# Chunked attention and a quadratic-ReLU network on one core: q and k of the first tiles loaded four tokens to a partition and turned in 64x64 blocks, the first stages in another order, copies of weights issued later

## The chip, the core and the metric

One NeuronCore of a Trainium2 chip runs the whole program. Its engines each work through a queue of their own: TensorE multiplies matrices (PE in the profile, its weight loads PEld), VectorE (DVE) and ScalarE (ACT) work element by element, GpSimd (POOL) and SyncE (SP) mostly issue DMAs. They wait for one another by semaphores. The metric is device time of one execution in microseconds (us), as the median over runs. Names in the profile leave buffer numbers out, so `q_sb` stands for both `q_sb0` and `q_sb1`.

## What is computed

```python
# q, k, v: (8, 8, 576, 64): batch, heads, tokens, head size; chunks of 64 tokens, 9 to a sequence
scores = scale * np.matmul(q_c, k_c.transpose(0, 1, 2, 4, 3))
scores = scores - np.max(scores, axis=-1, keepdims=True)
attn = np.exp(scores)
attn = attn / (np.sum(attn, axis=-1, keepdims=True) + 1e-09)
out = np.matmul(attn, v_c)
# x = the 8 heads side by side: (4608, 512); w_in (512, 2048), w_out (2048, 512)
h = x @ w_in
g = np.where(h >= 1, h, np.where(h <= -1, 0.0, (h + 1) ** 2 / 4))
return g @ w_out
```

Each token attends only to the 64 tokens of its own chunk. The weights come as 64-bit floats and are read as pairs of 32-bit words.

## The kernel before

The 4608 tokens are nine tiles of 512 (`t` = 0 to 8): the first 512 tokens of each of the eight sequences, and one tile (`t` = 6) of the eight last chunks. Attention handles two heads at a time, `g` = 0 to 3. The network goes through the hidden size in 16 steps `j` of 128.

**Network.** Every float32 operand of the large products is split into a high and a low part (`xh` and `xl`, `gh` and `gl`, two halves of `weight`), and three products take the place of one. `ffn_in(t, j)` is 12 matmuls of 128x512, `ffn_out(t, j)` is again 12, three for each of the four output banks. Tiles 0 to 2 go so. From tile 3 on the tiles go in pairs: `ffn_quad` computes the hidden layer of a pair with seven products of mixed operands for each two steps; it keeps one tile's result, and sends the other's to memory (`hold`), from where `recall` fetches it for the pair's second tile. The mixed weights are made in tiles 1 and 2 by `mix_weights` and written to memory by `to_mixed`, on the POOL queue. Three of the seven are plain parts of `weight` and need no arithmetic; the kernel before issues these three copies ahead of the arithmetic.

**Attention.** `attn_turn` transposes q and k of two heads, `scores_of` multiplies them in 64x64 blocks, `attn_softmax` subtracts the maximum, takes exp and divides by the sum; `attn_turn_back` transposes the result and `values_of` multiplies it with v; `attn_split` copies it into `xh` and `xl`. For `t` = 0, and for `g` = 0 and 1 of `t` = 1 (`by_row`), the turning is done on TensorE: `flip` is four transposes of 128x128 against an identity matrix into one bank, for q and then for k, and ACT copies each bank to memory on chip. Later tiles are turned on DVE. The loads of these early q and k (`load_rows`, `load_halves`) put one token of each chunk on a partition, so every piece of memory that a DMA reads is one token of one head, 64 floats or 256 bytes.

**Order.** Nothing is issued in the order of the code. `Plan.add` notes every piece of work with its engine, an assumed cost, and what it reads and writes. `Plan.emit` then plays it through, giving a free engine its ready piece of lowest rank, and so writes one fixed queue for each engine. Where TensorE would be idle in that play before the network starts, it adds fillers: multiplications of the identity with itself (L1105), into banks that are not in use yet. They are instructions like any other: once in the queue they run, whether or not TensorE would have had to wait. The whole queue of before has 45 fillers.

**First stages.** `first_loads` gives the order of the loads for `t` = 0, the k of `g` = 0 and 1 on the ACT queue and the rest on SP. A loop then turns, scores and normalises `g` = 0 to 3, with the way back and the values two steps behind. The weights of the first three steps are prepared (`prepare`: word pairs to high and low parts, three operations of ACT and three of DVE each) after that in rank.

**Outputs.** `store` copies a finished output bank to a buffer, by ACT for `s` = 0 and 2 and by DVE for `s` = 1 and 3, and SP sends it. From tile 2 on the buffers are the four `tmp`, taken in turn. `ffn_quad` takes from the same four for what `hold` sends to memory.

## Time and profile before

| what | value |
|---|---|
| runs | 829.47, 829.10, 827.03 us; median 829.1 |
| the profiled execution | 828.9 us, its span 827.1 us |
| granted TensorE clock | 1.000 |
| moved | 146.80 MB in 278683 packets, 243152 of them under 512 bytes |
| TensorE by lines | L700 about 582 us, L880 about 273 us, L665 about 203 us of summed durations, which overlap |
| work for the first attention tile | up to about 30 us |
| last matmul starts | 822.94 us |

Durations of neighbouring matmuls overlap, so what a matmul costs is read from the start of one to the start of the next. In rows of the timeline the columns are: start in us, us covered by the row, engine, line, operation, what it writes and reads, shape, number of records; and in brackets how long the engine sat idle before it and what ended that. A float32 matmul outside the transpose mode leaves two records in the trace (the first 12 fillers are x24).

### The profile page before, as it was taken

How to read it: one execution, taken by the hardware profiler on the slowest of the kernel's cores; microseconds unless marked ns; L12 is line 12 of the kernel's file. 1: busy time of each engine (PE TensorE's matmuls, PEld its weight loads, DVE VectorE, ACT ScalarE, POOL GpSimd, SP SyncE). 2: the span in 40 equal slices, each digit the busy share in tenths (PEclk: the TensorE clock that was granted, in tenths of full speed). 3: DMA queues.
4: the chain of work that ended last, by engine and by line, in shares of the span. 5: the costliest groups of instructions: out<-in, count | busy, mean ns of one | idle time of the engine just before them, and what ended most of it. 6: DMA issues, size and time to landing. Idle time of an engine off the chain costs nothing.

```text
span 827.1 us, 15446 instructions
## 1 busy us (share of the span) xinstructions
PE 819.0 (99%) x5786; PEld 676.7 (82%) x5786; DVE 563.2 (68%) x965; ACT 422.5 (51%) x723; POOL 153.8 (19%) x278
## 2 busy tenths in 40 slices
PE   9999999999999999999999999999989999999998
PEld 8778878888888888888888888888878888888886
DVE  4889998857778888786787748775756254454422
ACT  5899965444445465455464344544544254454422
POOL 1222112222221111112122111121122121121220
PEclk9999999999999999999999999999999999999999
DMA  9998886554697546979597738875663264552432
GB/s 203 285 314 294 247 195 156 137 124 101 170 242 150 124 102 175 260 179 262 167 226 231 175 108 214 216 190 188 164 223 95 63 207 157 168 169 86 157 98 77
DMA packets 278683, 146.80 MB, mean 177 GB/s; under 512 B 243152, under 2 KB 251600, under 8 KB 278608
## 3 DMA queue, kind: packets, MB, share of 16 engines
q1 hardware_dynamic: 251584, 61.25, 33.7%
q0 software_dynamic: 24768, 83.90, 31.0%
q10 hardware_dynamic: 2256, 0.66, 0.5%
q8 instruction: 46, 0.75, 0.4%
q14 instruction: 29, 0.24, 0.1%
HBM read 101.71 MB, written 36.70 MB: 167 GB/s over the span
## 4 chain that ended last, share of the span: by engine, by line
PE 88%; DMA 4%; issue 2%; DVE 2%; SPq 2%; POOL 1%; ACT 0%; ACTq 0%; POOLq 0%; DVEq 0%
PE ps_o L700 43%; PE ps_h L880 26%; PE ps_h L665 13%; PE ps_a L478 2%; PE ps_h L496 2%; PE ps_a L700 1%; DMA words_wo<-in_moe_w_out_dram 1%; DMA v_sb<-in_v_dram 1%; DMA q_sb<-in_q_dram 1%; SPq L409 1%; DMA held<-tmp 1%; SPq L359 1%; DMA k_sb<-in_k_dram 1%; PE ps_a L436 0%; PE ps_o L665 0%
## 5 line engine op out<-in xcount | busy, mean ns | idle before, releaser
L700 PE MATMUL ps_o<-parts_wo,gh 128*128 128x512 f32 x1120 | 347.9, 392 | 2.2 <-DVE tmp L727 2.2
L700 PEld LDWEIGHTS ps_o<-parts_wo,gh 128*128 128x128 f32 x1120 | 208.6, 188 | 46.2 <-DVE tmp L727 2.8
L700 PE MATMUL ps_o<-parts_wo,gl 128*128 128x512 f32 x560 | 218.4, 390 | 0.0
L880 PE MATMUL ps_h<-big_wi,big_wi 128*128 128x512 f32 x720 | 172.3, 389 | 0.0
L880 PEld LDWEIGHTS ps_h<-big_wi,big_wi 128*128 128x128 f32 x720 | 135.2, 188 | 28.0
L665 PE MATMUL ps_h<-xh,parts_wi 128*128 128x512 f32 x376 | 125.4, 394 | 0.1
L686 DVE TENSOR_TENSOR gl<-r,gh 128x512 fp32r<-128x512 f32 x120 | 82.4, 687 | 60.9 <-ACT gh L685 60.1
L700 PEld LDWEIGHTS ps_o<-parts_wo,gl 128*128 128x128 f32 x560 | 105.2, 188 | 22.4 <-DVE gl L686 0.3
L685 ACT CAST gh<-r 128x512 fp32r<-128x512 f32 x120 | 74.2, 619 | 96.0 <-PE ps_o L700 55.8
L811 POOL DMA_DIRECT2D big_wi<-mixed x84 | 44.9, 535 | 264.1 <-PE ps_h L880 251.7
L665 PEld LDWEIGHTS ps_h<-xh,parts_wi 128*128 128x128 f32 x376 | 70.6, 188 | 16.1 <-DVE r L676 0.5
L665 PE MATMUL ps_h<-xl,parts_wi 128*128 128x512 f32 x188 | 73.6, 391 | 0.4 <-DVE xl L614 0.4
L894 ACT ACTIVATE tmp<-big_wi 128x512 f32<-128x512 f32 x48 | 30.3, 632 | 71.4 <-DVE big_wi L889 70.0
L880 PE MATMUL ps_h<-xh,big_wi 128*128 128x512 f32 x192 | 63.5, 390 | 0.0
L672 ACT ACTIVATE r<-ps_h 128x512 f32<-128x512 f32 x47 | 27.9, 597 | 43.6 <-PE ps_h L665 43.4
L889 DVE TENSOR_TENSOR big_wi<-ps_h,big_wi 128x512 f32<-128x512 f32 x48 | 32.9, 685 | 19.0 <-PE ps_h L880 13.8
L898 DVE SCALAR_TENSOR_TENSOR tmp<-big_wi,tmp 128x512 f32<-128x512 f32 x48 | 33.2, 692 | 15.9 <-ACT tmp L897 15.8
L676 DVE SCALAR_TENSOR_TENSOR r<-ps_h,r 128x512 f32<-128x512 f32 x47 | 32.1, 682 | 16.1 <-ACT r L675 15.9
L880 PEld LDWEIGHTS ps_h<-xh,big_wi 128*128 128x128 f32 x192 | 36.1, 188 | 7.7 <-DVE e L889 0.2
L665 PEld LDWEIGHTS ps_h<-xl,parts_wi 128*128 128x128 f32 x188 | 35.3, 188 | 7.7 <-DVE xl L614 0.7
L761 POOL DMA_DIRECT2D mixed<-e x32 | 17.2, 543 | 127.2 <-ACT e L790 127.2
L904 POOL DMA_DIRECT2D held<-tmp x48 | 26.4, 550 | 72.6 <-DVE tmp L898 72.5
(150 smaller groups left out, 1030.9 us busy)
## 6 DMA issues: line engine op xcount, KB each, us to landing
big_wi<-mixed POOLq DMA_DIRECT2D x84, 512.0 KB, 4.0
held<-tmp POOLq DMA_DIRECT2D x48, 256.0 KB, 3.8
words_wi<-in_moe_w_in_dram SPq DMA_DIRECT2D x16, 512.0 KB, 6.6
words_wo<-in_moe_w_out_dram SPq DMA_DIRECT2D x16, 512.0 KB, 7.5
out_dram<-tmp SPq DMA_DIRECT2D x31, 256.0 KB, 3.3
aT_both<-qT_both SPq DMA_DIRECT2D x112, 64.0 KB, 2.8
v_sb<-in_v_dram SPq DMA_DIRECT2D x52, 128.0 KB, 3.7
q_sb<-in_q_dram SPq DMA_DIRECT2D x104, 64.0 KB, 3.5
```

What stands on the lines that cost most here:

```text
L665: nc.tensor.matmul(out=ps, lhsT=weight["wi", j][:, half, kc * P:(kc + 1) * P], rhs=x, start=(kc == 0 and i == 0), stop=(kc == KC - 1 and i ...
L672: plan.add("act", 0.48, lambda: nc.scalar.activation(out=r, in_=ps, func=AF.Relu, bias=0.5, scale=0.5), (pkey,), (rkey,))
L676: plan.add("dve", 0.6, lambda: nc.vector.scalar_tensor_tensor(out=r, in0=ps, scalar=1.0, in1=r, op0=ALU.max, op1=ALU.min), (pkey,), (rkey,))
L685: plan.add("act", 0.52, lambda: nc.scalar.copy(out=gh, in_=r), (rkey,), (ghkey,))
L686: plan.add("dve", 0.6, lambda: nc.vector.tensor_tensor(out=gl, in0=r, in1=gh.bitcast(F32), op=ALU.subtract), (rkey, ghkey), (glkey,), port ...
L700: nc.tensor.matmul(out=acc, lhsT=x[:, cols], rhs=weight["wo", j][:, half, :], start=(j == 0 and i == 0), stop=(j == NF - 1 and i == 2),)
L811: plan.add("pool", 0.65, lambda: nc.gpsimd.dma_start(out=place_of(f"wi{slot}").bitcast(F32), in_=mixed[u]), keys, (f"wi{slot}_0", f"wi{slo ...
L880: nc.tensor.matmul(out=bank, lhsT=w[:, c:c + P], rhs=x()[:, kc, :], start=start and kc == 0 and k == 0, stop=kc == 1 and k == 2, skip_grou ...
L889: plan.add("dve", 0.6, lambda: nc.vector.tensor_tensor(out=out(), in0=bank, in1=x(), op=ALU.add), (key, xkey), (out_key,))
L894: plan.add("act", 0.5, lambda: nc.scalar.activation(out=r, in_=h(), func=AF.Relu, bias=0.5, scale=0.5), (hkey,), (rkey,))
L898: plan.add("dve", 0.6, lambda: nc.vector.scalar_tensor_tensor(out=r, in0=h(), scalar=1.0, in1=r, op0=ALU.max, op1=ALU.min), (hkey,), (rkey,))
L904: plan.add("pool", 0.65, lambda: nc.gpsimd.dma_start(out=held[j], in_=r), (rkey,), (f"held{j}",), lag=2.1, moving=0.8)
```

## The change

**Loading and turning.** For the tiles of `by_row`, `load_rows` now loads q and k of two heads in one DMA: partition `p` gets tokens 4p to 4p + 3 of both heads, so pieces of 1024 bytes. `flip_rows` turns q and k together by 32 multiplications of 64x64 blocks with a 64x64 piece of the identity, into a pair of banks. One copy for each of q and k then puts the tokens back in order: it reads the bank in order and writes every fourth element. Two of the eight copies of `t` = 0 (k of `g` = 0 and 1) are DVE's, the others ACT's. v of `t` = 0 and of the first half of `t` = 1 goes in two DMAs as other tiles do.

**Order.** The loop over the first stages is replaced by `in_turn`, a list written out; softmax is cut in two (`attn_exp`, `attn_norm`), and the preparing of the first weights stands in the list. `first_loads` is reordered, and k of `g` = 0 and 2 goes on ACT's queue. Softmax and the turn back of later bursts get 22 places less of priority (`plan.behind`).

**Late copies and one buffer.** `mix_weights` issues its three plain copies after the arithmetic. `store` puts bank `s` = 3 of tiles 3, 5 and 7 into the one `e` buffer instead of a `tmp`.

```diff
+        rows = src[BATCH[t], 2 * g:2 * g + 2, :T, :].rearrange("h (p r) d -> p h (r d)", r=NS)
+        queue.dma_start(out=dst.rearrange("p (h e) -> p h e", h=2), in_=rows)
...
+    def flip_rows(pair, q_rows, k_rows):
+        for r in range(NS):
+            for n, x in enumerate((q_rows, k_rows)):
+                for a in range(2):
+                    for h in range(2):
+                        rows, at = slice(a * C, (a + 1) * C), h * HALF + r * D
+                        to = n * HALF + r * C
+                        nc.tensor.matmul(
+                            out=pair[h * D:(h + 1) * D, a, to:to + C],
+                            lhsT=x[rows, at:at + D], rhs=ident[rows, rows], start=True, stop=True,
+                        )
...
-            plan.add("pe", 0.45, lambda src=src, ps=ps: flip(ps, src), (skey,), pkeys, columns=T,
-                     lag=0.0)
-            copy = plan.add(
-                "act", 0.48, lambda ps=ps, dst=dst: nc.scalar.copy(out=dst, in_=ps),
+        plan.add("pe", 0.75, lambda: flip_rows(pair, *(src for (_, src), _ in sides)),
+                 [skey for (skey, _), _ in sides], pkeys, columns=1024, lag=0.0)
+        for n, (_, (dkey, dst)) in enumerate(sides):
+            by_dve = (t, g, n) in COPIED
+            eng = nc.vector.tensor_copy if by_dve else nc.scalar.copy
+            turned[n] = plan.add(
+                "dve" if by_dve else "act", 0.6 if by_dve else 0.48,
+                lambda n=n, dst=dst, eng=eng: eng(
+                    out=dst.rearrange("p (a u r) -> p a r u", a=2, r=NS),
+                    in_=pair[:, :, n * HALF:(n + 1) * HALF].rearrange("p a (r u) -> p a r u", r=NS),
+                ),
                 pkeys, (dkey,), lag=late(t, 1.5),
             )
...
+            elif t >= PAIRED and (t - PAIRED) % 2 == 0 and s == NS - 1:
+                okey, o = e_bufs[0]
...
-        ("q", 0), ("k", 0), ("q", 1), ("k", 1), ("q", 2), ("k", 2), ("wi", 0), ("q", 3), ("k", 3),
-        ("v", 0), ("v", 1), ("wi", 1), ("v", 2), ("v", 3),
+        ("q", 0), ("k", 0), ("q", 1), ("k", 2), ("k", 1), ("q", 2), ("wi", 0), ("v", 1),
+        ("q", 3), ("k", 3), ("v", 0), ("wi", 1), ("v", 2), ("v", 3),
...
+    in_turn = (
+        "T0 S0 A0 T1 S1 N0 A1 N1 T2 S2 B0 V0 T3 S3 A3 A2 X0 B1 V1 N2 X1 B2 N3 B3 "
+        "V2 V3 W0 W2 X2 X3 W1"
+    )
...
+        plan.behind = 22
         for at in then:
             attn_softmax(*at)
         if then:
             attn_turn_back_pair(then)
+        plan.behind = 0
```

In the list, T turns q and k, S makes scores, A is maximum to exp, N is the sum and the division, B turns back, V makes values, X splits, and W prepares weights.

What this does to the queues is seen at three places. First the start of TensorE's queue. The names `q_sb`, `first_wi` and so on are buffers of q and k, `ps_o` and `ps_a` banks, `kT` and `qT_both` the turned tiles. Before:

```order
L1105 MATMUL ps_h_107<-ident 128x128 x12
L436 MATMUL ps_o_106<-ident,k_sb_72 128x128 x4
L1105 MATMUL ps_h_107<-ident 128x128
L436 MATMUL ps_o_105<-ident,q_sb_70 128x128 x4
L1105 MATMUL ps_h_107<-ident 128x128 x4
L478 MATMUL ps_a<-kT_78,qT_both 64x64 x16
L436 MATMUL ps_o_106<-ident,k_sb_73 128x128 x4
L436 MATMUL ps_o_105<-ident,q_sb_71 128x128 x4
L1105 MATMUL ps_h_107<-ident 128x128 x4
L478 MATMUL ps_o_103<-first_wo_116 64x64 x16
```

After, on the same engine from the same place (three more pairs of L439 rows follow each pair shown):

```order
L1130 MATMUL ps_h_106<-ident 128x128 x11
L439 MATMUL ps_o_103<-ident,q_sb_70 64x64 x4
L439 MATMUL ps_o_103<-ident,k_sb_72 64x64 x4
...
L1130 MATMUL ps_h_106<-ident 128x128 x5
L493 MATMUL ps_a<-kT_78,qT_both 64x64 x16
L439 MATMUL ps_o_103<-ident,q_sb_71 64x64 x4
L439 MATMUL ps_o_103<-ident,k_sb_73 64x64 x4
...
L1130 MATMUL ps_h_106<-ident 128x128 x8
L493 MATMUL ps_o_104<-first_wo_115 64x64 x16
```

Eight transposes have become 32 block products for each `g`, one burst instead of two, and the scores of one `g` stand directly ahead of the turning of the next. The fillers are 49 in the whole queue, 11 of them ahead of the first turning.

Second, ACT's queue where the last attention results of the first tile are copied (`first_wi` under L581 and L601 takes `aT`, the turned-back softmax of `g` = 2 and 3; `words_wo` is the first block of `w_out` as loaded). Before:

```order
L581 COPY first_wi_113<-ps_o_106 128x512
L613 CAST xh_0_85<-ps_o_103 128x2x4x64
L338 CAST parts_wi_455<-tmp_101 128x512
L613 CAST xh_0_87<-ps_a 128x2x4x64
L320 ACTIVATE tmp_102<-words_wi_353 128x512
L326 ACTIVATE words_wi_353<-words_wi_353 128x512
L581 COPY first_wi_113<-ps_o_106 128x512
L320 ACTIVATE tmp_99<-words_wo_355 128x512
```

After:

```order
L321 ACTIVATE tmp_101<-words_wi_355 128x512
L633 CAST xh_0_85<-ps_o_104 128x2x4x64
L327 ACTIVATE words_wi_355<-words_wi_355 128x512
L321 ACTIVATE tmp_99<-words_wo_365 128x512
L601 COPY first_wi_112<-ps_o_103 128x512
L327 ACTIVATE words_wo_365<-words_wo_365 128x512
L339 CAST parts_wi_552<-tmp_102 128x512
L601 COPY first_wi_112<-ps_o_103 128x512
```

The first reading of `words_wo` stood behind the last of these copies and now stands ahead of both.

Third, DVE's queue at the end of tile 5 (L898 and L921 end what `hold` sends off, L727 and L749 are `store`). Before:

```order
L898 SCALAR_TENSOR_TENSOR tmp_99<-big_wi_161,tmp_99 128x512
L686 TENSOR_TENSOR gl_97<-r_93,gh_95 128x512
L727 COPY tmp_101<-ps_o_106 128x512
L686 TENSOR_TENSOR gl_98<-big_wi_161,gh_96 128x512
L727 COPY tmp_99<-ps_o_103 128x512
L686 TENSOR_TENSOR gl_97<-r_94,gh_95 128x512
```

After:

```order
L921 SCALAR_TENSOR_TENSOR tmp_102<-big_wi_160,tmp_102 128x512
L706 TENSOR_TENSOR gl_98<-r_94,gh_96 128x512
L706 TENSOR_TENSOR gl_97<-r_93,gh_95 128x512
L749 COPY tmp_100<-ps_o_103 128x512
L749 COPY e_80<-ps_o_104 128x512
L706 TENSOR_TENSOR gl_98<-big_wi_160,gh_96 128x512
```

The second copy of an output bank went into the buffer of the last held result, `tmp_99`; now it goes into `e_80`, and stands directly behind the first.

More of the change, by code (lines that the diff above doesn't have):

```diff
@@ L238, in bank_pair @@
         return psum.tile([P, 2, T], F32, name=name)
-    o_pair, a_pair = bank_pair("ps_o23"), bank_pair("ps_a")
-    o_banks = buffers(psum, "ps_o", 2) + [(f"ps_o{2 + b}", o_pair[:, b, :]) for b in range(2)]
+    o_pairs, a_pair = [bank_pair("ps_o01"), bank_pair("ps_o23")], bank_pair("ps_a")
+    o_pair = o_pairs[1]
+    o_banks = [(f"ps_o{b}", o_pairs[b // 2][:, b % 2, :]) for b in range(4)]
     a_banks = [(f"ps_a{b}", a_pair[:, b, :]) for b in range(2)]
@@ L355, in load_rows, with by_half @@
     def load_rows(dst, src, t, g, queue):
-        dst = dst.rearrange("p (c d) -> p c d", d=D)
-        for j in range(2):
-            queue.dma_start(
-                out=dst[j * C:(j + 1) * C],
-                in_=heads_rows(src, t, 2 * g + j).rearrange("c p d -> p c d"),
-            )
-    def load_halves(dst, src, t, g, queue):
-        dst = dst.rearrange("p (u r d) -> p u r d", r=2, d=D)
-        for j in range(2):
-            rows = heads_rows(src, t, 2 * g + j).rearrange("(r u) p d -> r p u d", r=2)
-            for r in range(2):
-                queue.dma_start(out=dst[j * C:(j + 1) * C, :, r, :], in_=rows[r])
+        rows = src[BATCH[t], 2 * g:2 * g + 2, :T, :].rearrange("h (p r) d -> p h (r d)", r=NS)
+        queue.dma_start(out=dst.rearrange("p (h e) -> p h e", h=2), in_=rows)
     def by_row(t, g):
         return t < TURNED or t == TURNED and g in ROWED
+    def by_half(t, g):
+        return t == TURNED and g not in ROWED
     def load_blocks(dst, src, t, g, queue):
@@ L464, in attn_turn @@
             if t == 0:
-                turned[n] = copy
+                ended[0] = turned[n]
     def scores_of(t, g):
@@ L475, in product @@
             rows = slice(half * C, (half + 1) * C)
-            at = i * HALF + n * C if t == TURNED and not by_row(t, g) else (2 * n + i) * C
+            at = (i * HALF + n * C if by_half(t, g)
+                  else (n // 2 * 4 + 2 * i + n % 2) * C if by_row(t, g) else (2 * n + i) * C)
             at = slice(at, at + C)
@@ L560, in attn_softmax, with attn_norm @@
         ), (), (ekey,))
+    def attn_norm(t, g):
+        skey, sm = room("sm", sm_bufs, t, g)
+        ekey, e = e_room(t, g)
+        e3 = e.rearrange("p (n k) -> p n k", k=C)
         def norm():
@@ L567, in attn_softmax @@
         plan.add("dve", 1.05, norm, (ekey,), (skey,))
-        on_pool = t < 1
+        on_pool = t == 0 and g in POOLED
         eng = nc.gpsimd if on_pool else nc.vector
@@ L771, in mix_weights @@
         keys = {n: (f"wi{n}_0", f"wi{n}_1") for n in (i, j)}
-        for n, kc, which in ((i, 0, 1), (i, 1, 2), (j, 1, 4)):
-            to_mixed(m, which, [(None, keys[n], lambda n=n, kc=kc: weight["wi", n].bitcast(F32)[:, :, kc * HALF:(kc + 1) * HALF])])
         def whole(n, dst):
@@ L799, in mix_weights @@
                 ])
+        for n, kc, which in ((i, 0, 1), (i, 1, 2), (j, 1, 4)):
+            to_mixed(m, which, [(None, (*keys[n], bkey), lambda n=n, kc=kc: weight["wi", n].bitcast(F32)[
+                :, :, kc * HALF:(kc + 1) * HALF
+            ])])
     RING = 5
```

73 lines of the change are left out of this document (35 added, 38 removed).

## Prediction

> **What bounds the kernel now.** I read the page first, then the waits of TensorE, then its timeline at the start and at the places where it waits.
>
> ```profile
> span 827.1 us, 15446 instructions
> PE 819.0 (99%) x5786; PEld 676.7 (82%) x5786; DVE 563.2 (68%) x965; ACT 422.5 (51%) x723; POOL 153.8 (19%) x278
> ```
> ```profile
> PE ps_o L700 <- DVE tmp L727: 2.2, 1, 2.2
> PE ps_h L1105 <- POOL ident masks.py:199: 1.4, 1, 1.4
> PE ps_h L665 <- DVE xl L614: 0.4, 1, 0.4
> PE ps_a L436 <- DMA q_sb<-in_q_dram: 0.2, 1, 0.2
> ```
>
> The second fence is the whole list of what TensorE waited for (us in total, times, longest): 4.2 us in an execution of 827.1. The kernel is bound by TensorE's own queue, and the time of the changed one is a sum over that queue plus whatever waits are left. Of the four waits, 1.4 us is for the identity matrix and stays. The other three, 2.8 us together, are all that a better order can take away; anything more must come out of instructions that are no longer in the queue. There are such instructions: the fillers and turnings of the first 30 us.
>
> ```profile
> 1.36 5.09 PE L1105 MATMUL ps_h<-ident 128*128 128x128 f32 x24 [1.36 <-POOL ident masks.py:199]
> 6.29 0.60 PE L436 MATMUL ps_o<-ident,k_sb 128*128 128x128 f32 x4
> ...
> 11.54 1.09 PE L436 MATMUL ps_o<-ident,first_wi 128*128 128x128 f32 x8
> 12.47 1.06 PE L1105 MATMUL ps_h<-ident 128*128 128x128 f32 x8
> 13.46 0.69 PE L478 MATMUL ps_a<-first_wi,first_wo 64*64 64x64 f32 x32
> 14.08 0.66 PE L436 MATMUL ps_o<-ident,e 128*128 128x128 f32 x4
> ...
> 17.67 0.69 PE L496 MATMUL ps_a<-aT_both,v_sb 64*64 64x64 f32 x32
> 18.18 0.65 PE L478 MATMUL ps_o<-first_wi,first_wo 64*64 64x64 f32 x32
> 18.76 0.66 PE L436 MATMUL ps_o<-ident,kT 128*128 128x128 f32 x4
> ...
> 29.61 0.68 PE L665 MATMUL ps_h<-xh,parts_wi 128*128 128x512 f32 x2
> 30.64 0.50 PE L665 MATMUL ps_h<-xl,parts_wi 128*128 128x512 f32 x1 [0.36 <-DVE xl L614]
> ...
> 34.65 0.39 PE L665 MATMUL ps_h<-xh,parts_wi 128*128 128x512 f32 x1
> ```
>
> In these rows TensorE goes from one row straight into the next: fillers cover all waiting. At 34.65 the first three steps of the network (36 matmuls) are done. Whether the changed kernel reaches the same point earlier is the first question.
>
> **Term 1, the first 35 us: +0.5 us.** All of it is counted from starts of rows.
> - Turning. Eight transposes take 12.47 - 11.54 = 0.93 us for one `g`. A burst of 16 block products, alone, takes 14.08 - 13.46 = 0.62; two in a row take 18.76 - 17.67 = 1.09 (0.51 and 0.58). `flip_rows` is 32 products of the same size, in float32 and not in the transpose mode, so two such bursts: 1.09, or +0.16 for each of four `g`: +0.6. Ends for this price: 0.62 (if the products with the identity take one record instead of two, as the 128x128 transposes do) and 1.24 (no gain from following each other). I take 1.09, since the rows of the scores have the same shape and type.
> - Joins. By the order, S0 and S1 are followed directly by a turning, and S2, turning 3 and V0 stand in a row: four joins of bursts where before had one (V0 with S3). A join saves 0.62 - 0.51 = 0.11: three more give -0.35.
> - Fillers: 11 instead of 12 ahead of the first turning, 38 instead of 33 after it. Four fillers take 13.46 - 12.47 = 0.99, so 0.25 each: five more are +1.25. One less at the start, between two records at the running rate and two at 5.09 / 24 = 0.21, is -0.2 to -0.4; I take -0.3.
> - The wait at 30.64. From 29.61 to 30.64 two matmuls took 1.03 where two take 0.46 otherwise (0.23 each): 0.57 lost. In the new order values, splits and weights of steps 0 and 1 are done further ahead of it: -0.6.
> - Sum: 0.6 - 0.35 + 1.25 - 0.3 - 0.6 = +0.6. A last few tenths of idling ahead of the turnings of `g` = 2 and 3 go too; I take +0.5, with 0 and +1.2 as ends. The longer queue is also the reason why I charge no new waits here: the copies out of the banks now run on two engines, yet TensorE comes to the scores no earlier than before, so ACT and DVE gain time on it.
>
> The loads gain as well, but nothing waits for them there. Stretches of the windows view:
>
> ```profile
> 5.00:10.00 5.00, 5.00 (x68) 4.81 (x68) 0.83 (x2) 1.48 (x3) 0.00 (x0) 1.00 1.34 212
> 40.00:50.00 10.00, 10.00 (x44) 7.79 (x43) 8.64 (x16) 9.63 (x18) 2.23 (x3) 1.00 1.02 352
> ```
>
> The last two columns are the busy share of the DMA engines and GB/s: 212 with the 256-byte pieces of q and k, 352 with pieces of 1 and 4 KB. q and k of tile 0 are 2 MB, so by these rates they take 5.7 us instead of 9.4. The first turning still starts after 11 fillers, near 6 us, because they are in the queue.
>
> **Term 2, the two turnings in tile 1: +0.6 us.** These stand among the network's matmuls.
>
> ```profile
> 53.12 0.63 PE L436 MATMUL ps_a<-ident,q_sb 128*128 128x128 f32 x4 [0.18 <-DMA q_sb<-in_q_dram]
> ```
> ```profile
> 56.34 0.60 PE L436 MATMUL ps_a<-ident,k_sb 128*128 128x128 f32 x4
> 56.70 0.48 PE L665 MATMUL ps_h<-xh,parts_wi 128*128 128x512 f32 x1
> ```
> ```profile
> 65.76 0.39 PE L700 MATMUL ps_o<-parts_wo,gl 128*128 128x512 f32 x1
> 66.08 0.69 PE L478 MATMUL ps_a<-kT,qT_both 64*64 64x64 f32 x32
> 66.70 0.73 PE L700 MATMUL ps_o<-parts_wo,gh 128*128 128x512 f32 x2
> ```
>
> Four transposes cost 56.70 - 56.34 = 0.36, and the matmul behind covers 0.48 instead of 0.39: 0.45 each time, 0.9 for q and k. A block burst costs 66.70 - 65.76 = 0.94 less the 0.23 that the matmul ahead takes anyway, and the pair behind covers 0.73 instead of 0.62: 0.82. The second 16 products add 0.51: 1.33. So +0.43 for each of two `g`, +0.9, less the wait of 0.18 and its slow restart, together 0.3: +0.6. Ends: -0.1 if the products are as cheap as the transposes, less the wait, and +1.2.
>
> **Term 3, the output buffer: -2.5 us.**
>
> ```profile
> 614.59 1.21 PE L496 MATMUL ps_h<-aT_both,v_sb 64*64 64x64 f32 x64
> 617.98 0.73 PE L700 MATMUL ps_o<-parts_wo,gh 128*128 128x512 f32 x2 [2.18 <-DVE tmp L727]
> ```
> ```profile
> 617.23 0.69 DVE L727 COPY tmp<-ps_o 128x512 f32<-128x512 f32 x1 [2.74 <-DMA held<-tmp]
> ```
> ```profile
> 611.74 0.54 POOL L939 DMA_DIRECT2D r<-held  x1 [4.02 <-DVE gl L686]
> 612.27 0.55 POOL L904 DMA_DIRECT2D held<-tmp  x1
> ```
>
> Read from the top: TensorE waits 2.18 us for DVE to empty the fourth bank; DVE waits 2.74 us for the buffer `tmp`, from which a held result is still on its way to memory; and that DMA was issued only at 612.27, because on POOL's queue it stood behind a `recall` that waited for DVE. With `e` as the buffer the copy needs the bank alone. The last reader of `e` stands ahead of the copy on DVE's own queue. DVE can then copy at about 614.5, where it fell idle (617.23 - 2.74), and be done near 615.2; the burst covers TensorE until 614.59 + 1.21 = 615.8. What is late next is the burst's own end, so all 2.18 us go. At the end of tile 7 the same copy costs a little too:
>
> ```profile
> 780.42 0.39 PE L700 MATMUL ps_o<-parts_wo,gl 128*128 128x512 f32 x1
> 780.86 0.73 PE L700 MATMUL ps_o<-parts_wo,gh 128*128 128x512 f32 x2
> ```
>
> 0.44 from start to start instead of 0.23, and 0.11 behind it: -0.3. At the end of tile 3 TensorE does not wait.
>
> **The rest: -0.2 us, mostly cover.** The three late copies of each `mix_weights` stand behind its arithmetic on POOL. They are issued there while POOL otherwise waits, and leave the first 110 us, in which the DMA engines are fullest (1.02 above); a few tenths of weight parts coming late near 43 us should go with that: -0.2. If that cover failed, each us by which a mixed weight comes late would be one of TensorE's; POOL's busy share of 19% leaves room. Softmax at 22 places less of priority comes later on DVE and ACT. What hides that is the time from one burst to the next, four steps of 24 matmuls or 22 us in tile 2; the list of waits names no turned-back softmax now, and without cover it would cost what it comes late.
>
> **Sum.** 0.5 + 0.6 - 2.5 - 0.2 = -1.6 us. The profiled execution took 828.9 us, 0.2 under the median of 829.1, with 1.8 us around its span: 828.9 - 1.6 = 827.3. I forecast **827.3 us**. What a measurement of this kernel can tell from no change is about 0.3%, 2.5 us; the forecast lies inside it.
>
> **Rivals.**
> 1. *Cheap blocks.* The products with the identity take half of what I charge (0.62 for a `g`). That takes 4 x 0.47 = 1.9 us from term 1, of which waits for the copies give back about half, and 0.9 from term 2: 825.4. For it: the 128x128 transposes, also products with the identity, leave one record each (x4 for four at 6.29). Against it: the block products at 13.46 leave 32 for 16, and the new ones are issued as those are.
> 2. *Slow copies.* The copies out of the turned banks write every fourth element. No row of this trace writes so; the nearest read every second word.
> ```profile
> 28.03 0.66 ACT L320 ACTIVATE tmp<-words_wo 128x512 f32<-128x512 f32 x1 [1.24 <-DMA words_wo<-in_moe_w_out_dram]
> ```
> ```profile
> 7.59 0.58 ACT L461 COPY qT_both<-ps_o 128x512 f32<-128x512 f32 x1
> ```
>  At most some 0.08 more than a plain copy, so I charge nothing. If a copy took twice its 0.58, S0 and S1 would wait about 0.4 us together, and S2 and S3, whose two copies both stand on ACT, about 1 us each: +2.3, so 829.6. The Trainium skill (SBUF — State Buffer, "Door 1: The DMA port swizzle") says that on-chip memory has lines of 16 bytes and that an access which moves on to a new line each time pays a penalty; a step of four float32 is just that, so by this rule the copies would be slow and the time this rival's. No run here shows it yet.
> 3. *A queue that waits for a load: slower than before.* ACT now reads the first block of `w_out` ahead of both last copies of `aT`. Before, this load came at 28.03 after 1.24 us of waiting. If it came no earlier now, the first copy would start at 28.03 + 0.56 and end near 29.2, and V2 would start near 29.4 instead of about 26 (the queue's rows up to V2 at the prices of term 1): 3.4 us, so 830.7. It decides from about 24.7 us of landing on. Against it: with q and k 3.7 us shorter on the DMA engines it should land near 23 or 24. The same can happen to q and k of tile 1, `g` = 1. Before, TensorE waited for them at 53.12; by the order they are now wanted 42 matmuls after the 36th, near 35.2 + 42 x 0.227 = 44.7. What lies ahead of them is shorter by 3.7 us for tile 0, by 1.9 us for their own 1 MB at the two rates, and by the copies of weights that went to memory meanwhile:
> ```profile
> mixed<-parts_wi POOLq DMA_DIRECT2D x6, 256.0 KB, 6.9
> ```
>  1.5 MB in the first 40 us, 4.4 us at 352 GB/s. So I estimate a landing near 53.0 - 10.0 = 43.0, not 2 us ahead of need.
> 4. *The stall only moves.* One `tmp` less taken per pair shifts which buffer every later store gets. If another store then meets a held result, the 2.5 us come back: 829.8. Against it: the first three stores of a tile meet held results of older steps, for which nobody waited.
>
> **How the numbers follow.** Forecast 0.58 (its terms move by about 1 us either way, so a quarter of it lies below 826.5); cheap blocks 0.10; slow copies 0.11; a late load 0.12; moved stall 0.09. Low end: cheap blocks, 825.4, rounded up to 825.6, as only half of that case lies lower. High end: the late load, 830.7. Faster by over 0.3%: 0.25 x 0.58 + 0.10 = 0.25. Slower by over 0.3%: a late load on top of another rival, 0.08. Within: 0.67.
>
> **What would show it.** L439 rows: 1.1 us for 64 records in a burst, or half. The gap from a turning to its scores: filled by fillers (right) or idle with ACT L472 as releaser (rival 2, whose copies then last over 0.8). The 36th network matmul: near 35.2 by term 1. The wait at the end of tile 5 gone, and no wait for DVE L749 in the list. ACT L321 on `words_wo` idle beyond 24.7, or a turning that waits for `q_sb` or `k_sb`: rival 3. The prediction is wrong if TensorE's queue is not the bound of the first 30 us, or if a wait of over 2 us appears that is in none of these.

## The result and the profile after

| | before | after |
|---|---|---|
| median | 828.6 us (6 runs, 827.0 to 832.6) | 840.06 us (6 runs, 838.88 to 840.37) |
| ratio of the two | | 1.0134, 95% interval 1.0115 to 1.0152 |
| profiled execution, span | 828.9, 827.1 us | 838.88, 837.1 us |

The changed kernel is 11.4 us slower, and the forecast was 827.3 with 830.7 as its upper end. The page of after, TensorE's busy time and the number of its instructions:

```profile
span 837.1 us, 16069 instructions
PE 823.3 (98%) x6130; PEld 679.2 (81%) x6130; DVE 563.2 (67%) x967; ACT 423.6 (51%) x721; POOL 153.7 (18%) x278
```

344 more matmuls and as many weight loads, and 13.8 us in which TensorE does nothing, where it was 8.1. What it waited for (us in total, times, longest):

```profile
PE ps_o L493 <- issue: 2.6, 1, 2.6
PE ps_o L720 <- DVE tmp L749: 1.8, 2, 1.0
PE ps_h L1130 <- POOL ident masks.py:199: 1.4, 1, 1.4
PE ps_a L493 <- DVE kT L472: 1.0, 1, 1.0
PE ps_o L493 <- ACT first_wi L472: 0.8, 1, 0.8
PE ps_h L511 <- DVE big_wi L912: 0.5, 1, 0.5
PE ps_a L493 <- ACT first_wi L472: 0.4, 1, 0.4
PE ps_o L493 <- DVE first_wo L472: 0.4, 1, 0.4
```

The wait of 2.2 us at the end of tile 5 has gone. In its place stand four waits of the scores (L493) for copies (L472), 2.6 us together, and one of 2.6 us named "issue", which means that the profile shows nothing for which TensorE waited. To see where the time went, take the start of the n-th matmul of the network, counted from 0, in both traces and subtract (n = 36 is the first one behind the first three steps, called the 36th below; this is worked out from the traces, since no view prints it):

```
n                        36     72    456   2376   2424   last   end of span
start before, us       34.65  42.86 142.36 607.02 621.53 822.94   827.1
after minus before     +7.41  +7.39  +7.69 +10.89  +9.01  +9.02   +10.0
```

So 7.4 us of the 10.0 are lost before the network's 36th matmul, 0.3 in the turnings and the rest of tiles 1 and 2, 3.2 in small pieces up to the end of tile 5, where 1.9 come back, and 1.0 after the last matmul. The timeline of TensorE through the worst place shows in one piece what happened:

```profile
16.72 0.69 PE L493 MATMUL ps_a<-first_wi,first_wo 64*64 64x64 f32 x32 [0.41 <-ACT first_wi L472]
...
20.68 0.68 PE L493 MATMUL ps_o<-first_wi,first_wo 64*64 64x64 f32 x26 [0.78 <-ACT first_wi L472]
23.94 0.34 PE L493 MATMUL ps_o<-first_wi,first_wo 64*64 64x64 f32 x6 [2.58 <-issue]
...
24.89 0.67 PE L685 MATMUL ps_h<-xh,parts_wi 128*128 128x512 f32 x1
25.35 0.63 PE L685 MATMUL ps_h<-xl,parts_wi 128*128 128x512 f32 x1
25.77 0.63 PE L685 MATMUL ps_h<-xh,parts_wi 128*128 128x512 f32 x1
26.20 2.57 PE L1130 MATMUL ps_o<-ident 128*128 128x128 f32 x12
```

The burst of the fourth scores stops after 26 of its 32 records, although everything that it reads is there. It goes on 2.6 us later, and then TensorE is slow: 0.42 to 0.46 from one network matmul to the next instead of 0.23, and 2.5 us for six fillers that took 1.4 before (x12 at 19.26). The windows view names it, in the column behind POOL: the granted clock, 0.66 in these 5 us, 1.00 ahead of them. The trace's own clock records are sharper: 0.50 from 25.02 to 28.43 (3.41 us), and 1.00 on either side.

```profile
24.00:29.00 5.00, 5.00 (x46) 4.54 (x49) 3.97 (x9) 1.77 (x3) 1.47 (x2) 0.66 1.12 378
```

And the copies out of the turned banks, from the timeline of ACT and DVE:

```profile
6.75 1.09 ACT L472 COPY qT_both<-ps_o 128x512 f32<-128x512 f32 x1 [3.67 <-PE ps_o L439]
7.86 1.05 DVE L472 COPY kT<-ps_o 128x512 f32<-128x512 f32 x1 [7.86 <-ACT qT_both L472]
```

Each takes 1.05 to 1.15 us where the plain one took 0.58 on ACT, and DVE's does not run beside ACT's but behind it: the program itself makes it wait for ACT's semaphore.

### The profile page after: what moved, and what is told of

Read it like the earlier page. It is cut to its first block, busy times and chain, and to the rows that moved or that the text cites. A ratio compares the mean times of both kernels' runs of the same rounds, so it can differ in the third digit from the quotient of the medians.

```text
span 837.1 us, 16069 instructions
## 1 busy us (share of the span) xinstructions
PE 823.3 (98%) x6130; PEld 679.2 (81%) x6130; DVE 563.2 (67%) x967; ACT 423.6 (51%) x721; POOL 153.7 (18%) x278
## 4 chain that ended last, share of the span: by engine, by line
PE 87%; DVE 5%; ACT 4%; DMA 2%; issue 1%; SPq 1%; POOL 0%; DVEq 0%; POOLq 0%; ACTq 0%
PE ps_o L720 41%; PE ps_h L903 27%; PE ps_h L685 12%; PE ps_h L511 2%; PE ps_a L493 2%; PE ps_a L720 1%; DMA words_wo<-in_moe_w_out_dram 1%; DMA r<-held 1%; PE ps_o L1130 1%; SPq L376 1%; DVE tmp L332 1%; PE ps_h L1130 1%; ACT tmp L321 1%; DVE gl L706 1%; PE ps_o L439 1%
## 5 line engine op out<-in xcount | busy, mean ns | idle before, releaser
L921 DVE SCALAR_TENSOR_TENSOR tmp<-big_wi,tmp 128x512 f32<-128x512 f32 x48 | 33.1, 689 | 13.5 <-ACT tmp L920 13.4
```

The lines of the kernel that those rows point to most:

```text
L921: plan.add("dve", 0.6, lambda: nc.vector.scalar_tensor_tensor(out=r, in0=h(), scalar=1.0, in1=r, op0=ALU.max, op1=ALU.min), (hkey,), (rkey,))
```

## The experiments

Three theories for the first 42 us: **A**, the copies are slow and stand one behind the other; **B**, TensorE ran out of instructions, because a turning has 128 of them where eight transposes had 16; and, as it turned out that both could hold, a third cause in the new order. Theory **C**, formed after the run `store`, is about the rest of the kernel: a buffer that comes free earlier lets the planner deal out DVE's other work anew. (In what was expected of `order`, C still stands for the third cause, the new order itself.)

**Copies that write in order** (`plain`). This run leaves the putting back in order out, so its scores belong to other tokens.

```diff
-                    out=dst.rearrange("p (a u r) -> p a r u", a=2, r=NS),
-                    in_=pair[:, :, n * HALF:(n + 1) * HALF].rearrange("p a (r u) -> p a r u", r=NS),
+                    out=dst.rearrange("p (a x) -> p a x", a=2),
+                    in_=pair[:, :, n * HALF:(n + 1) * HALF],
```

> The copies out of the turned banks write in order instead of every fourth element (so the scores belong to other tokens); queues, engines and counts stay. Theory A (the 9 us at the start are the slow copies and what waits for them): ACT's copies take 0.58 instead of 1.09 us, DVE's 0.69 instead of 1.05, each of the four scores starts 0.5 to 1 us earlier, the idle stretch of 2.6 us in the fourth scores goes, and the 36th network matmul comes 5 us or more earlier than in the changed kernel (near 37). Theory B (TensorE stood still for want of instructions, since the new turning has 128 of them for 16, and came back at a low clock): copies are shorter as above, but the stall stays, 36th matmul near 40 to 41, total 837 to 839.

840.0 us (one run; before 830.8 beside it). The timeline of its copies, and TensorE's rows that end a wait between 12 and 25 us:

```profile
7.14 0.69 DVE L472 COPY kT<-ps_o 128x512 f32<-128x512 f32 x1 [7.14 <-PE ps_o L439]
7.87 0.58 ACT L472 COPY qT_both<-ps_o 128x512 f32<-128x512 f32 x1 [4.79 <-DVE kT L472]
```
```profile
12.86 0.47 PE L493 MATMUL ps_o<-first_wo 64*64 64x64 f32 x17 [0.36 <-issue]
17.13 1.10 PE L439 MATMUL ps_o<-ident,first_wi 64*64 64x64 f32 x60 [0.47 <-issue]
23.93 0.48 PE L493 MATMUL ps_o<-first_wi,first_wo 64*64 64x64 f32 x6 [3.70 <-issue]
```

The copies are as short as plain ones, no score waits for one any more, and nothing is gained: TensorE comes earlier to the same instruction, stands there longer (3.7 us) and goes on at 23.93, in the changed kernel at 23.94. With slow copies or with quick ones, something else set that moment. That the stall stays is what B expected and A did not. The 36th matmul comes at +8.27 (42.9 us), later than either expected; the low clock lasts here from 22.44 to 29.27.

**Copies that read every fourth element** (`gather`): the same two patterns, with `a r u` turned into `a u r` on both sides, so that the writing is in order.

> The copies read every fourth element out of the banks and write in order, so the result is the same. If the price lies on the writing side (16-byte steps in on-chip memory), copies take 0.58 and 0.69 us and the run is like the one with copies in order; if it is any 16-byte step, 1.05 to 1.15 us as in the changed kernel and the time stays at 839 to 840.

838.0 us (one run). The copies take 0.59 and 0.69, so the price lies on the writing side alone:

```profile
6.94 0.69 DVE L472 COPY kT<-ps_o 128x512 f32<-128x512 f32 x1 [6.94 <-PE ps_o L439]
7.66 0.59 ACT L472 COPY qT_both<-ps_o 128x512 f32<-128x512 f32 x1 [4.59 <-DVE kT L472]
```

The stall is there again (3.2 us), and the 36th matmul is at +7.45.

**Wider products** (`wide`). Here q and k get a bank of their own each.

```diff
-                        nc.tensor.matmul(
-                            out=pair[h * D:(h + 1) * D, a, to:to + C],
-                            lhsT=x[rows, at:at + D], rhs=ident[rows, rows], start=True, stop=True,
+                    nc.tensor.matmul(
+                        out=ps[h * D:(h + 1) * D, r * P:(r + 1) * P],
+                        lhsT=x[:, at:at + D], rhs=ident, start=True, stop=True,
```

> Turning by 16 products of 128x64 with the identity for 32 of 64x64: 64 instructions of TensorE for one g instead of 128, q and k each in a bank of its own, copies still with a step of four on writing. Theory A: only the waiting of DVE's copy for ACT's goes (0.3 to 1 us for each of g = 0 and 1), copies stay at 1.09; total 838 to 839. Theory B: 192 instructions fewer ahead of the fourth scores; the stall there shortens or goes, total 831 to 835.

836.1 us (one run), a little over B's range and under A's. There is no "issue" in the list of waits. But 8 of these products, for q alone, take 0.92 us where 32 small ones take 1.09 for q and k together, so a turning is 1.9 us instead of 1.1, and the 36th matmul comes 4.0 us late for 7.4. The two copies now overlap, and each waits for TensorE alone:

```profile
6.84 1.09 ACT L470 COPY qT_both<-ps_o 128x512 f32<-128x512 f32 x1 [3.76 <-PE ps_o L436]
7.71 1.08 DVE L470 COPY kT<-ps_o 128x512 f32<-128x512 f32 x1 [7.71 <-PE ps_o L436]
```

So the waiting of DVE for ACT came from the pair of banks that both copies read: q and k of the changed kernel each lie in both banks of it. The Trainium skill (PSUM — Partial Sum Buffer, "PSUM bank collisions raise a hardware error") says that two engines must not be in one bank on the same partitions at the same time, two readers included, and that software has to keep them apart. These two rows, with a bank each, agree with it; none of them has two engines in one bank at once.

**More instructions in the kernel before** (`before_many`).

```diff
-            out=bank[:, :P], lhsT=ident, rhs=ident, start=True, stop=True
+            for r in range(2):
+                for h in range(2):
+                    nc.tensor.matmul(
+                        out=bank[h * C:(h + 1) * C, r * C:(r + 1) * C], lhsT=ident[:C, :C], rhs=ident[:C, :C],
```

> The kernel before, with each of its 45 fillers (a 128x128 product) replaced by four 64x64 products, 540 instructions more for TensorE in the first 30 us and about the same time in the array; nothing else is changed, copies are the plain ones. Theory B: a stretch of 1.5 to 4 us appears in the first 30 us in which TensorE waits for nothing that the profile shows, a fetch of instructions ends inside it, the matmuls behind run at a low clock, and the total rises by 3 to 8 us. Theory A: no such stretch, total within 1 us of before.

834.6 us, 3.8 over before. The stall appears in a kernel that has neither the new copies nor the new turning:

```profile
28.04 0.51 PE L1108 MATMUL ps_o<-ident 64*64 64x64 f32 x10
29.68 0.91 PE L1108 MATMUL ps_o<-ident 64*64 64x64 f32 x22 [1.13 <-issue]
```

Most of the 3.8 us are not due to it. TensorE works at about half its speed in this kernel until 13.8 us (told at the end), which puts it 3 us behind at 12 us, and the network's first matmul, still ahead of the stall, starts 4.5 us late; the 36th comes 6.9 us late. So this run shows that the stall needs neither copies nor turning, and only some 2.4 us at the 36th matmul can be the stall and the low clock behind it (0.50 from 30.85 to 34.26).

**Where the stalls are.** The page lists a DMA queue "instruction" (q8; packets, MB, share of the engines' time), here of after:

```profile
q8 instruction: 48, 0.79, 0.4%
```

48 packets of 16 KB, for 12,418 records of TensorE (matmuls, weight loads and a few others), 46 before: one for about 256. Counting these records from the start gives, for the kernels in which TensorE's list has a wait called "issue", worked out from the traces:

```
kernel        issued   stands still      packet landed  until it goes on
after            961   21.14 to 23.94        22.64            1.30
plain            449   12.28 to 12.86        11.44            1.42
plain            705   16.45 to 17.13        15.84            1.29
plain            961   20.01 to 23.93        22.69            1.24
gather           705   15.92 to 16.60        15.21            1.39
gather           961   19.48 to 22.85        21.63            1.22
order            961   22.25 to 24.68        23.20            1.48
longfill         449   15.05 to 15.62        14.16            1.46
longfill         705   20.52 to 21.82        20.62            1.20
before_many     1217   28.33 to 29.68        28.42            1.26
front_only       705   18.19 to 18.69        17.48            1.21
front_only       961   22.41 to 25.76        24.41            1.35
store           4289  244.62 to 245.58      244.18            1.40
```

Whatever instruction stands there, a stall comes at the 449th, 705th, 961st, 1217th or 4289th, which is 193 more than a multiple of 256 (`store` and `front_only` are told below), and it ends 1.2 to 1.5 us after a packet has landed. Other bursts can meet it too: at 245 us `store` has the products of attention for a later tile there. The opposite holds as well. The sixteen traces have 738 places that are 193 behind a multiple of 256; at the 714 that were reached 1.6 us or more after their packet had landed, the next record follows within 0.25 us. This is B in its sharpest form: TensorE runs on for 193 instructions behind each 256th, and then needs the next packet. In the changed kernel the 768th is issued at 17.88; the packet starts at 21.67 and lands at 22.64, among the loads that fill the DMA engines (their busy share is 1.07 from 20 to 25 us). The 193 instructions lasted 3.3 us there. Before, 768 is reached at 27.07, its packet lands at 29.87, and 961 is reached only at 44.39, so that a lag of 2.8 us costs nothing.

**The old order** (`order`): the list `in_turn` written as the loop of before had it.

```diff
-        "T0 S0 A0 T1 S1 N0 A1 N1 T2 S2 B0 V0 T3 S3 A3 A2 X0 B1 V1 N2 X1 B2 N3 B3 "
-        "V2 V3 W0 W2 X2 X3 W1"
+        "T0 S0 A0 N0 T1 S1 A1 N1 T2 S2 A2 N2 B0 V0 X0 T3 S3 A3 N3 B1 V1 X1 "
+        "B2 V2 X2 B3 V3 X3 W0 W1 W2"
```

> The changed kernel with its first stages in the order of the kernel before (scores, values and splits of one g after another; three preparations of weights last). Theory B (instructions): the turnings stay at 128 instructions each, but V0 and T3 no longer stand with S3 in a row, so that fewer dense bursts follow the 768th instruction; the stall stays within 1 us of 2.6 or moves to another burst, total 837 to 841. Theory A (copies; waits of the scores): S3 waits less since B0, V0 and X0 stand ahead of it, and the total falls to 835 to 837. Theory C (the new order itself costs the time): back near 831.

843.5 us, over the range of every theory; in this one run the old order does not bring the time back, so the new one is not shown to have cost it. The stall moved as B said, out of the scores into the values behind them, and to the same 961st instruction:

```profile
21.44 0.69 PE L493 MATMUL ps_o<-first_wi,first_wo 64*64 64x64 f32 x32 [0.61 <-ACT first_wi L472]
21.95 0.52 PE L511 MATMUL ps_a<-aT_both,v_sb 64*64 64x64 f32 x20
24.68 0.69 PE L511 MATMUL ps_a<-aT_both,v_sb 64*64 64x64 f32 x12 [2.21 <-issue]
```

**Longer fillers** (`longfill`): `rhs` is the identity four times over, 512 columns, and the planner's cost of a filler is four times as high, so that 16 take the place of 49.

> The changed kernel with fillers of 512 columns for 128, so some 17 in the place of 49: 130 instructions fewer in the first 30 us, of which 90 ahead of the fourth scores, the same work in the array. Turning and copies stay as they are. Theory B: TensorE gets past the fourth scores; the stall moves to the values behind them or goes, and is at most half as long; total 833 to 837. Theory A: S0 to S3 wait as before and the total stays at 838 to 840.

839.1 us. The stall of the 961st instruction is gone, and two others of 1.4 us together have come, inside turnings:

```profile
15.62 0.93 PE L439 MATMUL ps_o<-ident,first_wi 64*64 64x64 f32 x47 [0.36 <-issue]
...
21.82 0.57 PE L439 MATMUL ps_o<-ident,first_wi 64*64 64x64 f32 x23 [1.08 <-issue]
```

The total is A's, not B's. The 36th matmul is at +7.95. A filler of 0.85 us also stands in the way of what comes ready behind it, so this run shows where the stall goes and says little about time.

**Neither cause, and the copies alone** (`quick`, `quick_strided`). In `quick` only the upper halves of q and k are turned, as bfloat16: the same 32 products in 64 instructions and 0.38 us, with copies that write in order. `quick_strided` has the copies of the changed kernel.

```diff
-                            lhsT=x[rows, at:at + D], rhs=ident[rows, rows], start=True, stop=True,
+                            lhsT=x[rows, at:at + D].bitcast(BF16)[:, 1::2],
+                            rhs=ident[rows, rows].bitcast(BF16)[:, 1::2], start=True, stop=True,
```

> The changed kernel with the upper halves of q and k turned as bfloat16 (so q and k are cut to bfloat16): the same 32 products of 64x64 for one g, 64 instructions for 128, and shorter; and copies that read every fourth element and write in order. Theories A and B together explain the front: no wait in which nothing is shown, copies 0.59 and 0.69 us, the 36th network matmul 1.5 us earlier to 1 us later than before, total 828 to 832. If it comes 3 us or more later than before, a third cause lies in the first order (ACT and DVE, which then prepare weights all the time).

> The same with the copies of the changed kernel, which write every fourth element: the slow copies alone. Theory A says that they cost what rival 2 of the prediction reckoned or more: S0 to S3 wait 0.4 to 1 us each, the 36th network matmul comes 2 to 4 us later than in the run with the other copies. If fillers cover the copies, the difference is under 1 us, and nearly all of the 7.4 us belongs to the stall and the low clock behind it.

The 36th matmul comes at +0.22 in `quick` and at +1.51 in `quick_strided`; the changed kernel has +7.41. `quick` took 828.3 us beside a run of before with 829.4. The waits of `quick_strided` that `quick` has not, from its list:

```profile
PE ps_a L496 <- ACT qT_both L475: 1.0, 1, 1.0
...
PE ps_o L496 <- ACT first_wi L475: 0.8, 1, 0.8
...
PE ps_o L496 <- DVE first_wo L475: 0.4, 1, 0.4
PE ps_a L496 <- ACT first_wi L475: 0.4, 1, 0.4
```

So the slow copies alone make the scores wait 2.6 us, and cost 1.3 us at the 36th matmul, since `quick`, which comes earlier to everything, loses time of its own: 0.3 us at its 705th instruction and the rest in delays too short for the list. The other 5.9 us go with the turning's instructions, by an estimate 4 x 0.71 = 2.8 of them because a turning lasts 1.09 instead of 0.38.

The loss can also be added up in the trace of the changed kernel: the forecast's 0.5, 2.6 in waits for copies, 2.6 in the stall, and for the low clock, by an estimate, half of 3.41 us, 1.7. That is 7.4, as measured. Without waits for copies, and with the low clock counted from the end of the stall on, the same sum gives 7.2 for `gather` (7.45 measured) and 7.7 for `plain` (8.27); for `wide`, with four turnings 0.8 longer, 3.7 (4.0). It is not that exact: behind the same eleven fillers the first turning starts anywhere from 5.52 (the changed kernel) to 6.36 us (`quick`), and for `quick` the sum gives 0.5 - 2.8 and 0.8 in waits and stops, -1.5, where +0.2 was measured. So no third cause of 3 us is there, which was the mark set for it; one of 1 to 2 us is not excluded.

`quick_strided` ended at 835.2. 4.3 us of that were lost near 246 us, where TensorE waits for `aT_both` and `qT_both` and the granted clock then is 0.50 for 3.4 us. `rest` loses as much at the same place, `quick` less than half a microsecond, and why was not settled.

**Both remedies in full precision** (`wide_priced`): `wide` with copies that write in order, and 1.85, 0.59 and 0.69 as planned costs.

> The changed kernel with both suspects taken away: turning by 16 products of 128x64 (64 instructions for 128, 1.9 us for 1.1), copies that read every fourth element and write in order, and the planner's prices set to what the traces show. Theories A and B together: no wait in which nothing is shown, no wait for a copy over 0.3 us, the 36th network matmul 3 to 4 us later than before (four times 0.95 us of longer turning, less one filler or two), total 832.5 to 835. If it is still 6 us late or more, a third cause is in the first order.

839.0 us (median of 4, ratio 1.0109, 1.0092 to 1.0126), worse than expected. There is no "issue", and no wait for a copy. The 36th matmul comes 4.6 us late, and at the 72nd it is 8.8. With its new costs the planner wrote another order, in which TensorE waits for DVE in the network's first steps. Its windows (busy us of DVE and ACT are the third and fourth pair):

```profile
39.22 0.50 PE L683 MATMUL ps_h<-xh,parts_wi 128*128 128x512 f32 x1 [1.61 <-DVE r L694]
```
```profile
25.00:30.00 5.00, 5.00 (x91) 4.05 (x89) 4.93 (x11) 5.00 (x10) 1.74 (x2) 1.00 1.09 362
30.00:35.00 5.00, 5.00 (x53) 3.93 (x54) 4.82 (x9) 5.00 (x11) 0.27 (x1) 1.00 1.06 396
35.00:40.00 5.00, 3.39 (x15) 2.51 (x14) 5.00 (x11) 5.00 (x10) 0.00 (x0) 1.00 1.10 345
```

DVE and ACT are full there, 14.75 and 15.0 of 15 us; before they worked 11.9 and 12.0. A front that starts the network no earlier but crowds the weights' preparation has a bound of its own right behind.

**The other edits, in the kernel before.** `store` has the output buffer alone, `rest` also the late copies and the lower priority, `store_behind` the buffer and the priority, `store5` the buffer in tile 5 alone (`t == PAIRED + 2`); `front_only` is the changed kernel without all three.

> The kernel before with one part of the change, the output buffer for the fourth store of every other tile. By the prediction's term 3 the waits at 618 and 780 us go, 2.5 us; by the trace of the changed kernel, where the difference fell from 10.89 to 9.01 us at this place, 1.9 us. Expected 826.1 to 826.8 where before is 828.6. If the stall only moved (the rival), 828.6.

> The kernel before with everything that is not in the first 40 us or a turning: the output buffer, the late copies of weights to memory, and the lower priority of the softmax. If the loss of the changed kernel lies in the loading, turning and first order alone, this is no slower than the run with the output buffer, 826 to 827. If the late copies or the lower priority carry part of the 1 to 2 us that the changed kernel loses between tile 2 and tile 5, it is 827.5 to 828.5 and its trace shows the difference to the run with the output buffer growing between 150 and 450 us.

> The kernel before with the output buffer for the fourth store of tile 5 alone, so that only a dozen rows of the whole order change. Theory C (the buffer saves 1.9 us at 618 us, and what the kernel with all three buffers lost at 455 to 462 us came from DVE's order at the end of tile 3): 826.5 to 827.2 where before is 829, and no wait for DVE gl in TensorE's list. If the gain is given back in any case: 828.5 to 830.

> The kernel before with the output buffer in tiles 3, 5 and 7 and the lower priority of the softmax, without the late copies. Theory C: the splits of gl stand ahead of the softmax on DVE again, the 2.2 us at 455 to 462 us do not come, total 826.5 to 827.5. If the lower priority costs by itself, as softmax that comes late: 829 to 831, with waits for aT, e or kT in TensorE's list.

> The changed kernel without the output buffer, the late copies and the lower priority: only loading, turning and the first order are left. Its first 60 us are those of the changed kernel (36th network matmul 7 to 8 us later than before), the wait of about 1.9 us at the end of tile 5 is back. If the parts add up, the total is 840 less the 2 us by which the rest alone was slower than before: 837.5 to 839. If the rest helps the new front, over 840.

```
kernel         median, runs    ratio to before, 95% interval
store          830.7,  6       1.0021  (1.0001 to 1.0041)
rest           831.6,  6       1.0024  (0.9997 to 1.0051)
store_behind   830.8, 10       1.0008  (0.9988 to 1.0028)
store5         827.65, 12      0.9976  (0.9961 to 0.9990)
front_only     840.5,  4       1.0136  (1.0116 to 1.0155)
```

In `store` the 1.9 us at the end of tile 5 come as forecast (4.59 to 2.66 between n = 2376 and 2424), yet it is no faster than before. Its trace loses 2.2 us at 455 to 462 us, at the end of tile 3:

```profile
454.93 0.65 DVE L686 TENSOR_TENSOR gl<-big_wi,gh 128x512 fp32r<-128x512 f32 x1
```
```profile
455.64 0.50 PE L700 MATMUL ps_o<-parts_wo,gl 128*128 128x512 f32 x1 [0.71 <-DVE gl L686]
```

In the queue of before, this `gl` stands in the midst of the softmax (at 450.32 in its trace). In the queue of `store` the copy stands one place earlier, DVE's next operations are dealt out anew, and that `gl` falls behind the whole softmax and two turnings back, 15 operations in a row. Compared row by row as the traces have them (operations and names in order, without buffer numbers), DVE's queue of `store` and before's differ in 388 lines, that of `store5` in 14. `store5` has no such wait, loses nothing there (+0.72 from n = 888 to 2376), gains the 1.9 us, and at 827.65 us is the version that beats both kernels, if by 0.24% only. That is theory C. It is not all that `store` lost: its trace also has a wait of 1.5 us for `q_sb` in tile 1 (1.2 in `store5`, 0.2 before) and the stop of 1.0 us at the 4289th instruction. The lower priority in `store_behind` was to mend the same place, and its trace loses only 0.3 from 440 to 465 us; but DVE's queue differs in 809 lines, it loses 1.6 us in waits for `e` in the mixed products, and ends level with before. `rest` is not shown to differ from before. `front_only` is as slow as the whole change, so the three edits are worth about nothing next to the new front; the parts do not add up to better than 2 us.

## Why the prediction was wrong

**Term 1, the first 35 us: +0.5 forecast, +7.4 measured.** Its price of a turning was right: 6.61 - 5.52 = 1.09, so that rival 1, cheap blocks, fell. The first turning came 0.77 us earlier for the 0.3 of one filler less, but the same eleven fillers end at 5.52 to 6.36 us in the runs with them, so that is in part chance. What failed is the sentence "I charge no new waits here: the copies out of the banks now run on two engines, yet TensorE comes to the scores no earlier than before". Three things were wrong in it. The copies take twice the time. They run on two engines, but not at once, since both read the same two banks; these two faults together are the 2.6 us of waits. And TensorE's queue was taken as a row of durations that only other engines can hold up, when the instructions themselves have to arrive: that is the stall of 2.6 us and, by the estimate above, 1.7 of low clock, and no rival had it. The prediction named the sign of it, a wait of over 2 us that is in none of its cases, but as something that would be seen afterwards. The trace of before had a part of what was needed: 46 packets in the queue "instruction", while the change adds 112 instructions to each turning, 448 in 20 us. That TensorE stops 193 instructions behind a multiple of 256 could not be read from it, since nothing stops there.

**The slow copies, rival 2.** Its mechanism held: 1.05 to 1.15 us is the "twice its 0.58" that it supposed, and the four waits sum to 2.6 where it reckoned 2.3. They are spread otherwise, 1.3 for S0 and S1 where it had 0.4 and 1.2 for S2 and S3 where it had 2, so that the sums agree is in part luck. The forecast's own sentence, "at most some 0.08 more than a plain copy, so I charge nothing", is what fell. The row it leant on reads every second word; `gather` shows that reading is not where a step of four costs, writing is. The rule quoted from the Trainium skill (SBUF — State Buffer, "Door 1: The DMA port swizzle") agrees with the writing side, 1.09 for 0.58. It was quoted and then given 0.11.

**Term 2, the turnings of tile 1: +0.6 forecast.** From n = 72 to n = 456 the difference grows by 0.3. Both bursts last 1.10, and neither waited for q or k, so rival 3 did not come; `words_wo` was read at 30.54 without a wait.

**Term 3, the output buffer: -2.5 forecast, -1.9 measured at the place.** Of the 2.18 us at the end of tile 5, 1.9 went; the 0.3 at the end of tile 7 did not come. The step that failed is "At the end of tile 3 TensorE does not wait", from which nothing was charged: a buffer that comes free earlier let the planner move other work there (2.2 us in `store`, a wait of 1.0 in the changed kernel). Rival 4, that the stall moves, named the wrong mechanism (another store), but its price was that of `store`.

**The rest: -0.2 forecast, +3.2 between tile 2 and the end of tile 5.** Two waits in it are listed, 0.5 us for DVE at 366 us and 1.0 at the end of tile 3 for DVE's copy into `tmp`; the other 1.7 come in pieces too short for the list. Which of them belong to the priority, which to the late copies and which to chance was not separated. `quick` has the same three edits and loses 1.5 from n = 504 to n = 2376, so about half of it is not forced by them.

**The end: +1.0, not in any term.** From the last matmul to the end of the span it is 5.1 us in every kernel with the joined bank pair `ps_o0` and `ps_o1`, and 4.1 to 4.5 in those where they are apart, `wide` among them. After, and `wide`:

```profile
831.02 1.27 ACT L751 COPY tmp<-ps_o 128x512 f32<-128x512 f32 x2 [3.68 <-PE ps_o L720]
831.64 0.69 DVE L749 COPY tmp<-ps_o 128x512 f32<-128x512 f32 x1 [3.58 <-ACT tmp L751]
```
```profile
828.54 0.59 ACT L749 COPY tmp<-ps_o 128x512 f32<-128x512 f32 x1 [3.00 <-PE ps_o L718]
829.22 0.69 DVE L747 COPY tmp<-ps_o 128x512 f32<-128x512 f32 x1 [2.96 <-PE ps_o L718]
```

In the first, DVE's copy of bank `s` = 1 waits for ACT's of `s` = 0, not for TensorE, though they read different banks of the pair, and ACT's begins 0.94 us before the last matmul starts, for 1.61 in `wide`; in the second each waits for TensorE alone. So the waits of this program go by the tile, and a tile of two banks is one thing to them. The edit that made one tile of two banks stands at the top of the whole diff, outside the parts shown, as bookkeeping, and was not priced.

## What to carry to other kernels

Where a stage is made of many tiny matmuls, count instructions as well as microseconds: find the instructions that a burst adds, and see whether the stretch between one packet and the next still lasts longer than the packets' lag in that part of the kernel. A copy that reorders elements costs by the side that jumps, so let it read with the step and write in order, and give two engines that shall run side by side tiles and banks of their own. In a program whose order a planner writes, a freed buffer or a changed cost moves other work, so compare the whole queues before pricing an edit, and try the smallest form of it.

## What the runs showed of the hardware

- TensorE stood still at the 449th, 705th, 961st, 1217th or 4289th instruction, 193 behind a multiple of 256, in eight kernels, until 1.2 to 1.5 us after a packet of 16 KB; the packet landed up to 5.3 us after the instruction with a multiple of 256 (`front_only`, 19.15 to 24.41). Why it lagged so at 18 us and only 1.2 us at 9 was not settled; the loads on the same DMA engines are a likely reason, and no run took them away.
- About 1.1 us after TensorE went on from the stall of 2.6 us, the granted clock was 0.50 for 3.41 us. With the stalls of `plain` (3.7), `gather` (3.2) and `front_only` (3.1) it was 0.50 for 6.83 us from before their end on; behind the 1.1 us of `before_many` for 3.41; in `longfill`, with stalls of 0.4 and 1.1, not at all.
- A copy of 128x512 out of banks took 1.09 (ACT) and 1.05 (DVE) when it wrote every fourth element, 0.59 and 0.69 when it read so.
- The first clock record of a trace comes at 4.5 to 7.2 us, and until about then a filler takes some 0.4 us instead of 0.25. In `before_many`, with fillers of 64x64 products, it comes at 13.78, and four transposes of 128x128 took 1.04 us from start to start before it; eight took 1.02 after it, behind the same fillers. The profile prints a granted clock of 1.00 for both stretches. That the small products caused the late start fits, but was not tested by itself.

```profile
6.68 1.11 PE L436 MATMUL ps_o<-ident,k_sb 128*128 128x128 f32 x4
7.72 0.69 PE L1108 MATMUL ps_h<-ident 64*64 64x64 f32 x8
...
15.49 1.09 PE L436 MATMUL ps_o<-ident,first_wi 128*128 128x128 f32 x8
16.51 1.08 PE L1108 MATMUL ps_h<-ident 64*64 64x64 f32 x29
```
